# A chunked gated linear attention with an SSM projection: a reworked opening, and in the usual turns the third projection product moved ahead of the carried parts

## The chip, the cores and the metric

The kernel runs on one NeuronCore of a Trainium2 chip. It uses the five engines of that core: TensorE (PE, with its weight loads listed as PEld), VectorE (DVE), ScalarE (ACT), GpSimd (POOL) and SyncE (SP, which issues most transfers). The metric is the device time of one launch in microseconds (us); lower is better.

## What is computed

Two blocks in a row, all in float32. The first is a gated linear recurrence over 768 steps, for 4 batches and 8 heads of 48 numbers; the second projects its output to 2 × 512 columns, scans one half with a decay, gates it with the SiLU of the other half and projects back to 384 columns.

```python
for t in range(S):                                  # B, H, S, D = 4, 8, 768, 48
    state = alpha[:, :, t, :, None] * state + np.einsum('bhd,bhe->bhde', k[:, :, t], v[:, :, t])
    y[:, :, t] = np.einsum('bhd,bhde->bhe', q[:, :, t], state)
x = y.transpose(0, 2, 1, 3).reshape(B, S, H * D)    # (4, 768, 384)

proj = x @ w_in                                     # 384 x 1024
val, gate = proj[..., :512], proj[..., 512:]
a = np.exp(A_log)
for t in range(S):
    h = a[0, 0] * h + val[:, t, :]
    ys[:, t, :] = h
out = (gate * sigmoid(gate) * ys) @ w_out           # 512 x 384
```

The weights `w_in`, `A_log` and `w_out` come as numbers of 64 bits; the kernel turns their bits into float32 itself.

## The kernel before

The work is cut into 12 units of 256 steps (`GC`), three per batch. A unit `m` has an attention part and, one unit later, a projection part: turn `n` of the main loop does the attention of unit `m = n + 1` and the projection of unit `n`. The program's order is written out by hand (`manual_schedule`): each engine carries out its instructions in the order in which the code calls them, and semaphores make one engine wait for another.

**Attention of a unit.** alpha, k and q are loaded as `raw_a`, `raw_k`, `raw_q` (lines 410 and 421) and have to be turned, so that steps lie along the free axis. In the first units PE turns them by products with the identity (`turned`, line 694) or by transposes (lines 689 and 690) and ACT or DVE copy the result out of PSUM (`copy_turned`, lines 701 and 702); from unit 4 on DVE turns them by itself (`turn`, line 595). Two scans on DVE make the running products of alpha, forward (`scan_P`, L630) and backward (`scan_V`, L649); k and q are multiplied by them (`scaled_k` L614, `scaled_q` L605). Then PE does:

- `scores` (L744): k times q within each 64 steps, and k itself turned back; `masks` (L754 to L764) copies these out of PSUM, masked, by DVE, ACT and POOL;
- `values` (L778, for unit 0 `first_values`, L862): masked scores times v;
- `states` (L810): k times v, the step of the state for each 64 steps; `add_up` sums them on POOL (L828, L830), for the first units DVE does (L838, for unit 0 `first_states`, L879);
- `carried` (L791, for unit 0 `first_carried`, L870): q times the state at the start of each 64 steps, added to the values in the same PSUM banks (`y0`, `y1`);
- `join`: ACT copies the banks to `yst` (L904, L905), eight small transfers bring them into the layout `xT` (L907), ACT copies the rest straight (L909). For unit 0 `first_join` does this with four ACT copies.

**Projection of a unit.** `project(n, cc)` for `cc` from 0 to 3 makes 128 columns of values and 128 of gates on PE (L927, two PSUM banks), a scan with the decay on DVE (L932), a SiLU on ACT (L940) and their product on POOL (L942; DVE in the first turns). `output` is the last product (L956), its copy on ACT (L950) and two transfers.

**PSUM.** Four banks go round (`ps_mm`, tag `mm`), each given out again when its last reader is done: to the turned pieces, the second half of scores, each projection product (a pair), each output (a pair). Four more are named: `s0`, `s1`, `y0`, `y1`.

**Weights.** `load_w` brings the 64-bit numbers of `w_in` in three blocks (`units`: columns of product 0, of product 1, of products 2 and 3). `low(i)` (ACT, L544) takes the low word's bits, `convert(i)` the high word's on DVE (L553, L555) and adds the two on POOL (L557).

**The opening.** Before the loop unit 0 goes through alone: `keep_warm` (three products on zeros, L726), `alphas(0)` through the four named banks, q, k, `alphas(1)`, the scans, `turned(1, "k")`, scores, `turned(1, "q")`, masks, values, states, carried parts, join. Between them stand `low(0)`, `convert(0)`, `low(1)`, `convert(1)`. The loads on SP after the first ones are held back by a memset of one element on POOL (L1001) which stands behind the POOL add of `convert(0)`: `raw_a` of unit 2 must wait for it, and everything behind it on SP (the third weight block, k, q, alphas, v, the output weights) with it. `constants` (from L495) fills masks, paddings and the identity.

**A usual turn** (`n` from 2 on, the last `else` of the loop): scores and masks; product 0; values, states and three of the four sums (`second`); product 1; carried parts, values of the other half, join and the fourth sum (`third`), `load_v`; product 2; product 3; output of unit `n`. `go(count)` slips in steps of the DVE chain of unit `n + 2` (`products`).

Of the kernel before, what the change touches and what calls it, by code (L numbers as in the profile page):

```python
# [11 lines left out]
U32 = mybir.dt.uint32  # L12
# [334 lines left out]
def fast(  # L347
# [145 lines left out]
    def constants():  # L493
# [18 lines left out]
        for t in dS[0] + dS[1]:  # L512
            nc.vector.memset(t[:, :, :, D:64], 0.0)
        for t in sums:
            nc.vector.memset(t[:, :, D:64], 0.0)
        nc.vector.memset(K0[:, :, :, D:], 0.0)
# [21 lines left out]

    def low(i):
        bits, w = bits_of(i)  # L540
        r = p2.tile([C, UW], I32, tag="wr", name="wr")
        lows[i] = r.rearrange("p (a n) -> p a n", a=w.shape[1])
        halves = lows[i].bitcast(U16).rearrange("p a (n two) -> p a n two", two=2)
        nc.scalar.activation(halves[:, :, :, 0], bits[:, :, :, 0], AF.Copy, scale=2.0 ** -29)  # L544

    def convert(i):
        if i not in lows:
            low(i)
        bits, w = bits_of(i)
        r = lows.pop(i)  # L550
        halves = r.bitcast(U16).rearrange("p a (n two) -> p a n two", two=2)
        quarters = bits.rearrange("p a n two -> p a (n two)").bitcast(U16).rearrange("p a (n four) -> p a n four", four=4)
        nc.vector.tensor_scalar(out=w.bitcast(U32), in0=bits[:, :, :, 1], scalar1=3, scalar2=0x3FFFFFFF,  # L553
                                op0=ALU.logical_shift_left, op1=ALU.bitwise_and)
        nc.vector.tensor_scalar(out=halves[:, :, :, 1], in0=quarters[:, :, :, 3], scalar1=0xC000, scalar2=None,  # L555
                                op0=ALU.bitwise_and)
        nc.gpsimd.tensor_tensor(out=w.bitcast(I32), in0=w.bitcast(I32), in1=r, op=ALU.add)  # L557
# [125 lines left out]

    def turned(m, name, js, t):
        raw = steps_of(name, m)
        tp = t[:, 0:len(js) * C].rearrange("p (j x) -> p j x", j=len(js))
        if (m, name) in ((1, "k"), (1, "q"), (2, "a"), (3, "a")):
            for n, j in enumerate(js):
                nc.tensor.transpose(tp[:, n], raw[:, ds(ROW + j * D - 64, C)], ident)  # L689
                nc.tensor.transpose(tp[0:64, n], raw[:, ds(j * D, 64)], ident)  # L690
            return tp.rearrange("p j (c h) -> p h c j", h=4)
        for n, j in enumerate(js):
            for i in range(2):
                nc.tensor.matmul(tp[ds(64 * i, 64), n], raw[:, ds(i * ROW + j * D, 64)], ident,  # L694
                                 start=True, stop=True, skip_group_check=True)
        return tp.rearrange("p j (c h) -> p h c j", h=4)

    def copy_turned(to, js, tp, engine=None):
        place = by_runs(to)[:, :, :, js.start:js.stop]
        if engine:  # L700
            return engine.tensor_copy(out=place, in_=tp)
        return nc.scalar.activation(place, tp, AF.Copy)  # L702

    def turn_over(m, name, to, tags=(None, None)):
        size = NJ // len(tags)
        copies = []
        for n, tag in enumerate(tags):
            js = range(size * n, size * (n + 1))
            copy = copy_turned(to, js, turned(m, name, js, bank(tag)), nc.vector if n % 2 and tag else None)
            if tag:  # L710
                for other in copies[(n + 1) % 2::2]:
# [3 lines left out]
    def alphas(m, tags=(None, None)):  # L715
        turn_over(m, "a", by_place(als[m % 2])[:, :, 1:GP], tags)
# [31 lines left out]
    def masks(m):  # L748
        sc = [[t[:, 0:4 * (L + D)].rearrange("p (h x) -> p h x", h=4) for t in pair] for pair in scs.pop(m)]
        mb = mask[:, None, :]  # L750
        if m < NG:
            for c in range(G):
# [230 lines left out]
    alphas(0, ("s0", "s1", "y1", "y0"))  # L983
    tq = straighten(0, "q")
    tk = straighten(0, "k")
    alphas(1)
    P = scan_P(0)
    V = scan_V(0, P, False)
    halves = [range(0, NJ // 2), range(NJ // 2, NJ)]
    parts = [turned(1, "k", js, bank()) for js in halves]  # L990
# [22 lines left out]
    last = P[:, :, GC]  # L1013
    nc.scalar.activation(ratio[:, 0], last, AF.Copy, scale=1.0 / FIRST_PRODUCT)
    nc.scalar.activation(lower[:, :, 0], last, AF.Copy)
# [6 lines left out]
    first_carried((2, 3))  # L1022
    first_join()
    nc.scalar.activation(a_dec, a_log, AF.Exp)
# [26 lines left out]
    for n in range(N):  # L1051
# [70 lines left out]
        else:  # L1122
# [98 lines left out]
```

## Time and profile before

| | |
|---|---|
| median of 3 runs | 279.24 us (279.05 to 279.8) |
| profiled execution: its time | 279.67 us |
| its span, first to last instruction | 277.8 us |
| granted TensorE clock, mean | 1.000 |
| busy: PE, DVE, ACT, POOL | 271.7, 217.8, 110.3, 98.2 us |
| moved by DMA | 41.16 MB, 148 GB/s over the span |

The lines of the profile that follow are of three kinds. The chain of work that ended last has a start, a length and what ran. The timeline has a start, a length, engine, line of the code, operation, out<-in with shapes, a count, and in brackets the idle time before it with what ended it. A window over matmuls counts two rows for each product in float32. SPq is SyncE's queue of transfers; its length is that of the issue, and the landing is told apart.

### The profile page before, as it was taken

Reading aid. Unit: us, or ns where it says so; the run is one execution under the profiler, and the core shown is the slowest. Engines: PE = TensorE matmul, PEld = TensorE weight load, DVE = VectorE, ACT = ScalarE, POOL = GpSimd, SP = SyncE. Lnnn points to the kernel's source line nnn. Section 1 sums busy time; section 2 is a strip of 40 time slices with the busy share of each in tenths; the row PEclk is TensorE's granted clock in tenths of the full one; section 3 lists DMA queues with packets and bytes.
Section 4 is the critical chain, followed back from the end, with each engine's and each line's share of the span. In section 5 each row is a group of like instructions: output and inputs, shape, how many; then the busy total and the mean of one; then the engine's idle time right before and its main releaser. Section 6 shows DMA issues by size and latency. Waiting matters only on the chain.

```text
span 277.8 us, 9491 instructions
## 1 busy us (share of the span) xinstructions
PE 271.7 (98%) x4040; PEld 217.3 (78%) x4040; DVE 217.8 (78%) x281; ACT 110.3 (40%) x244; POOL 98.2 (35%) x105
## 2 busy tenths in 40 slices
PE   7999999999999999999999999999999999999995
PEld 5988987876688788788787787787787787787874
DVE  7889998898499599499499599499499598269640
ACT  2677763461325325325334334334343343341111
POOL 8131223230057155156156164164165163142000
PEclk9999999999999999999999999999999999999999
DMA  6949991935909739729659748829748711101101
GB/s 189 314 133 319 285 293 49 217 78 132 273 12 228 168 97 217 168 85 221 145 140 205 158 132 197 188 91 197 170 125 186 190 55 45 58 5 43 57 5 59
DMA packets 52462, 41.16 MB, mean 148 GB/s; under 512 B 27360, under 2 KB 50976, under 8 KB 52416
## 3 DMA queue, kind: packets, MB, share of 16 engines
q1 hardware_dynamic: 50768, 38.98, 55.3%
q10 hardware_dynamic: 1392, 0.99, 1.3%
q8 instruction: 32, 0.52, 0.8%
q0 software_dynamic: 256, 0.56, 0.7%
q14 instruction: 14, 0.11, 0.1%
HBM read 32.54 MB, written 4.72 MB: 134 GB/s over the span
## 4 chain that ended last, share of the span: by engine, by line
PE 94%; DVE 3%; DMA 1%; ACT 1%; issue 1%; SPq 0%; DVEq 0%; ACTq 0%
PE mm L927 47%; PE mm L956 20%; PE y L778 4%; PE y L791 4%; PE s L744 4%; PE mm L744 3%; PE s L810 3%; PE mm L1182 2%; DMA raw_a<-in_alpha_dram 1%; PE mm L694 1%; PE mm L689 1%; PE mm L690 1%; DVE V L649 1%; DVE P L630 1%; PE y L862 1%; PE s L694 1%
## 5 line engine op out<-in xcount | busy, mean ns | idle before, releaser
L927 PE MATMUL mm<-xT,w_in 128*128 128x256 f32 x576 | 133.4, 385 | 0.6 <-ACT xT L884 0.6
L927 PEld LDWEIGHTS mm<-xT,w_in 128*128 128x128 f32 x576 | 106.7, 190 | 17.1 <-issue 0.8
L956 PE MATMUL mm<-w_out,f_last 128*128 128x384 f32 x160 | 53.2, 486 | 0.0
L940 ACT ACTIVATE sg<-mm 128x256 f32<-128x256 f32 x48 | 18.4, 384 | 72.4 <-PE mm L927 71.9
L956 PEld LDWEIGHTS mm<-w_out,f_last 128*128 128x128 f32 x160 | 30.4, 190 | 19.1
L942 POOL TENSOR_TENSOR f_last<-sg,hh 128x256 f32<-128x256 f32 x36 | 34.3, 954 | 24.7 <-ACT sg L940 21.2
L830 POOL TENSOR_TENSOR sum<-sum,dS 128x192 f32<-128x192 f32 x30 | 31.2, 1039 | 18.2 <-ACT dS L818 16.8
L762 POOL TENSOR_TENSOR AK<-AK,mask 128x512 f32<-128x512 f32 x9 | 11.5, 1281 | 67.4 <-ACT AK L760 67.4
L649 DVE TENSOR_TENSOR_SCAN V<-al,ends 128x1028 f32<-128x1028 f32 x12 | 30.1, 2512 | 0.4
L932 DVE TENSOR_TENSOR_SCAN hh<-a_dec,hh,mm 128x256 f32<-128x256 f32 x32 | 23.1, 722 | 8.3 <-PE mm L927 8.1
L950 ACT ACTIVATE o_sb<-mm 128x384 f32<-128x384 f32 x22 | 10.8, 491 | 46.4 <-PE mm L956 46.4
L630 DVE TENSOR_TENSOR_SCAN P<-al,lower 128x1028 f32<-128x1028 f32 x12 | 27.5, 2292 | 0.4
L759 DVE TENSOR_TENSOR A<-s,mask 128x256 f32<-128x256 f32 x9 | 3.8, 425 | 29.5 <-PE s L744 29.5
L595 DVE STREAM_TRANSPOSE k<-raw_k 128x1024 f32<-128x1024 f32 x9 | 18.3, 2033 | 0.0
L595 DVE STREAM_TRANSPOSE q<-raw_q 128x1024 f32<-128x1024 f32 x9 | 18.1, 2016 | 0.0
L557 POOL TENSOR_TENSOR w_in<-w_in,wr 128x768 int32<-128x768 int32 x4 | 7.3, 1832 | 26.4 <-ACT al L702 9.5
L595 DVE STREAM_TRANSPOSE al<-raw_a 128x1024 f32<-128x1024 f32 x8 | 16.4, 2048 | 0.1
L605 DVE TENSOR_TENSOR Zq<-q,P 128x1024 f32<-128x1024 f32 (+1 forms) x14 | 15.0, 1070 | 0.3
L778 PEld LDWEIGHTS y<-AK,v 64*64 64x64 f32 x352 | 12.1, 134 | 3.6 <-issue 3.6
L614 DVE TENSOR_TENSOR Zk<-k,V 128x1024 f32<-128x1024 f32 (+1 forms) x14 | 14.7, 1050 | 0.1
L778 PE MATMUL y<-AK,v 64*64 64x64 f32 x352 | 14.5, 221 | 0.0
L778 PE MATMUL y<-A,v 64*64 64x64 f32 x352 | 14.5, 221 | 0.0
(158 smaller groups left out, 375.1 us busy)
## 6 DMA issues: line engine op xcount, KB each, us to landing
v<-in_v_dram SPq DMA_DIRECT2D x22, 192.0 KB, 4.0
out_dram<-o_sb SPq DMA_DIRECT2D x22, 192.0 KB, 4.2
raw_k<-in_k_dram SPq DMA_DIRECT2D x18, 184.0 KB, 3.6
raw_q<-in_q_dram SPq DMA_DIRECT2D x18, 184.0 KB, 4.2
raw_k<-in_k_dram SPq DMA_DIRECT2D x18, 176.0 KB, 4.1
raw_q<-in_q_dram SPq DMA_DIRECT2D x18, 176.0 KB, 4.3
raw_a<-in_alpha_dram SPq DMA_DIRECT2D x16, 184.0 KB, 5.2
raw_a<-in_alpha_dram SPq DMA_DIRECT2D x16, 176.0 KB, 5.1
```

The lines of the kernel that those rows point to most:

```text
L595: nc.vector.transpose(out=by_runs(to).rearrange("p h c j -> p h j c"), in_=raws[name][:, 0:4 * ROW].rearrange("p (h j d) -> p h j d", h=4, ...
L605: nc.vector.tensor_mul(Zqs[m % 2][:, ds(u0, n), :, D:].rearrange("p u h t -> p h u t"), t[:, :, at].rearrange("p h (u t) -> p h u t", t=L) ...
L630: nc.vector.tensor_tensor_scan(out=P, data0=al[:, 0:4 * GP], data1=lower.rearrange("p h t -> p (h t)"), initial=0.0, op0=ALU.mult, op1=ALU ...
L649: nc.vector.tensor_tensor_scan(out=V[:, ::-1], data0=al[:, 1:4 * GP + 1][:, ::-1], data1=ends.rearrange("p h t -> p (h t)")[:, ::-1], init ...
L744: nc.tensor.matmul(scs[m][c][i][ds(L * h, L), ds(p * (L + D), L + D)], Zk[rows, c, p, ds(h * L, L)], Zq[rows, u, p], start=True, stop=True ...
L778: nc.tensor.matmul(ys[m][i][ds(64 * s, 64), e, ds(c * C + h * L, L)], v_sb[rows, c, 4 * i + p, :], As[i][rows, c, p, :], start=across and ...
L830: nc.gpsimd.tensor_add(Ss[j][:, :, 0:D], Ss[j - 1][:, :, 0:D], part)
L927: nc.tensor.matmul((pv, pg)[vg], w_ins[cc][:, kk, vg, :], xT[:, kk, :], start=(kk == 0), stop=(kk == NK - 1))
L932: nc.vector.tensor_tensor_scan(out=hh, data0=a_dec[:, cc:cc + 1].to_broadcast([C, GC]), data1=pv, initial=prev_h[cc][:, GC - 1:GC] if n % ...
L940: nc.scalar.activation(sg, pg, AF.Silu)
L942: f = lambda: engine.tensor_mul(fs[n][cc], sg, hh)
L956: nc.tensor.matmul(os[c], fs[n][cc][:, ds(c * C, C)], w_outs[cc // 2][:, cc % 2, :], start=(cc == 0), stop=(cc == NI - 1))
```

## The change

Two parts. In the opening:

- `constants` leaves out the memsets of the paddings of `dS`, `sums` and `K0`; those of `sums` come back on POOL, later.
- `first_alphas` turns the alphas of unit 0 by 32 products of 64 × 64 (each with a quarter of the identity) in place of 16 of 128 × 64; four copies out as before, on ACT and DVE.
- `first_q` turns q of unit 0 with the order of the products changed: first all eight of the half that ACT's queue loads, then all eight of the other half.
- k of unit 0 and the alphas of unit 1 are turned by transposes (`turned_by_transpose`) in place of products.
- `turned(1, "k")` is split: one half before the scores, one after them. `turned(1, "q")` is split: one half after the states, one after the last carried parts.
- `masks` for unit 0 comes before all conversion of weights; `convert` is split into `high` (DVE), `low` (ACT) and `add_low` (POOL), and `low(0)` stands behind the copies of the scores, `high(1)` is done in two halves.
- The copies of P's last column (`ratio`, `lower`) on ACT come right after `scan_P(0)`.

In the usual turns `third(m)` and `load_v(m + 2)` come after `project(n, 2)` and its gating product; they came before.

```diff
@@ constants @@
-        for t in dS[0] + dS[1]:
-            nc.vector.memset(t[:, :, :, D:64], 0.0)
-        for t in sums:
-            nc.vector.memset(t[:, :, D:64], 0.0)
-        nc.vector.memset(K0[:, :, :, D:], 0.0)
@@ low, convert @@
+    def high(i, part=slice(None)):
         bits, w = bits_of(i)
+        halves = room(i)[1][:, part]
...
+        nc.vector.tensor_scalar(out=w.bitcast(U32)[:, part], in0=bits[:, part, :, 1], scalar1=3, scalar2=0x3FFFFFFF,
+                                op0=ALU.logical_shift_left, op1=ALU.bitwise_and)
+        nc.vector.tensor_scalar(out=halves[:, :, :, 1], in0=quarters[:, part, :, 3], scalar1=0xC000, scalar2=None,
+                                op0=ALU.bitwise_and)
+
+    def add_low(i):
+        w = bits_of(i)[1]
+        nc.gpsimd.tensor_tensor(out=w.bitcast(I32), in0=w.bitcast(I32), in1=lows.pop(i), op=ALU.add)
@@ turned @@
+    turned_by_transpose = ((0, "k"), (1, "a"), (1, "k"), (1, "q"), (2, "a"), (3, "a"))
...
-        if (m, name) in ((1, "k"), (1, "q"), (2, "a"), (3, "a")):
+        if (m, name) in turned_by_transpose:
@@ new @@
+    def first_alphas():
+        raw, to = steps_of("a", 0), by_runs(by_place(als[0])[:, :, 1:GP])
+        tps = [[bank(tag)[:, 0:NJ // 2 * 64].rearrange("p (j x) -> p j x", x=64) for tag in tags]
+               for tags in (("s0", "s1"), ("y1", "y0"))]
+
+        def turn_quarter(j, i, r):
+            rows = ds(64 * r, 64)
+            nc.tensor.matmul(tps[j // 4][r][ds(64 * i, 64), j % 4], raw[rows, ds(i * ROW + j * D, 64)],
+                             ident[rows, rows], start=True, stop=True, skip_group_check=True)
+
+        for j in range(2):
+            for r in range(2):
+                turn_quarter(j, 1, r)
+        for j in range(NJ):
+            for r in range(2):
+                turn_quarter(j, 0, r)
+                if j + 2 < NJ:
+                    turn_quarter(j + 2, 1, 1 - r)
...
+    def first_q():
+        raw, to = steps_of("q", 0), plain("q")
+        tps = [bank().rearrange("p (j x) -> p j x", x=C) for _ in range(2)]
+        for i in (1, 0):
+            for j in range(NJ):
+                nc.tensor.matmul(tps[j // 4][ds(64 * i, 64), j % 4], raw[:, ds(i * ROW + j * D, 64)], ident,
+                                 start=True, stop=True, skip_group_check=True)
...
@@ the opening @@
-    alphas(0, ("s0", "s1", "y1", "y0"))
-    tq = straighten(0, "q")
+    first_alphas()
+    tq = first_q()
     tk = straighten(0, "k")
     alphas(1)
     P = scan_P(0)
+    last = P[:, :, GC]
+    nc.scalar.activation(ratio[:, 0], last, AF.Copy, scale=1.0 / FIRST_PRODUCT)
+    nc.scalar.activation(lower[:, :, 0], last, AF.Copy)
     V = scan_V(0, P, False)
-    parts = [turned(1, "k", js, bank()) for js in halves]
+    part = turned(1, "k", halves[0], bank())
     for c in range(G):
         scaled_k(0, tk, V, c)
         scaled_q(0, tq, P, c)
-    scores(0)
     tk = plain("k")
-    for js, part in zip(halves, parts):
-        copy_turned(tk, js, part)
+    copy_turned(tk, halves[0], part)
+    for c in range(G):
+        scores(0, (c,))
+    part = turned(1, "k", halves[1], bank())
+    for c in range(G):
+        masks(0, (c,))
+    copy_turned(tk, halves[1], part)
+    high(0)
+    high(1, slice(0, None, 2))
     low(0)
-    parts = [turned(1, "q", js, bank()) for js in halves]
-    convert(0)
+    add_low(0)
     nc.gpsimd.memset(raws["a"][0:1, 0:1], 0.0)
     load_steps("a", 2, [nc.sync])
     load_w(units[2], nc.sync)
-    masks(0)
-    low(1)
     first_values(True)
     st = states(0)
-    convert(1)
+    tq = plain("q")
+    part = turned(1, "q", halves[0], bank())
     first_states(st)
-    tq = plain("q")
-    for js, part in zip(halves, parts):
-        copy_turned(tq, js, part)
...
+    low(1)
+    copy_turned(tq, halves[0], part)
+    high(1, slice(1, None, 2))
+    add_low(1)
+    for t in sums:
+        nc.gpsimd.memset(t[:, :, D:64], 0.0)
...
     first_carried((2, 3))
+    part = turned(1, "q", halves[1], bank())
     first_join()
+    copy_turned(tq, halves[1], part)
@@ the usual turn @@
-            third(m)
-            load_v(m + 2, nc.sync)
             go(1)
             f2 = project(n, 2)
             f2()
+            third(m)
+            load_v(m + 2, nc.sync)
```

More of the change, by code (lines that the diff above doesn't have):

```diff
@@ L548, in convert @@
             low(i)
[L549 to L557, printed above, removed]
+        high(i)
+        add_low(i)
     def check_w(i):
@@ L696, in turned @@
         return tp.rearrange("p j (c h) -> p h c j", h=4)
[L698 to L705, printed above, removed]
-        copies = []
[L707 to L711, printed above, removed]
+    halves = [range(0, NJ // 2), range(NJ // 2, NJ)]
@@ L718, in straighten, with turn_over, alphas @@
+    def turn_over(m, name, to):
+        for js in halves:
+            copy_turned(to, js, turned(m, name, js, bank()))
+    def alphas(m):
+        turn_over(m, "a", by_place(als[m % 2])[:, :, 1:GP])
     def straighten(m, name):
```

35 lines of the change are left out of this document (22 added, 13 removed).

## The prediction

> **What bounds the kernel now.** I read the page first (parts 1 and 4), then the chain of work, then the timelines by engine.
>
> ```profile
> PE 271.7 (98%) x4040; PEld 217.3 (78%) x4040; DVE 217.8 (78%) x281; ACT 110.3 (40%) x244; POOL 98.2 (35%) x105
> ...
> PE 94%; DVE 3%; DMA 1%; ACT 1%; issue 1%; SPq 0%; DVEq 0%; ACTq 0%
> ```
>
> TensorE (PE) is busy 98% of the span and carries 94% of the chain that ended last. A time can therefore only come out of work that PE does, or out of the few microseconds in which PE stands still. The chain over one usual turn (n = 8):
>
> ```profile
> 202.97 2.79 PE mm L927 x12
> 205.76 0.39 PE y L791 x16
> ...
> 207.08 5.38 PE mm L927 x24
> 212.46 5.16 PE mm L956 x16
> 217.62 0.93 PE s L744 x32
> ...
> 259.02 7.77 PE mm L927 x36
> ```
>
> Second projection product, carried parts (three pieces, 205.76 to 207.08), third and fourth product together, output, next scores: each piece begins where the last one ends. No usual turn has an idle PE. The idle time is in the opening.
>
> **The usual turns: third product ahead of the carried parts.** PE's instructions stay the same and change places: two products in one run (5.38) now stand before the carried parts, one (2.79) behind them. 2.79 + 5.38 is the sum on both sides, so PE's work is unchanged: 0. What could break this is a wait. The other engines in the same turn, by the timeline:
>
> ```profile
> 201.11 0.69 DVE L932 TENSOR_TENSOR_SCAN hh<-a_dec,hh,mm 128x256 f32<-128x256 f32 x1
> 201.72 0.38 ACT L940 ACTIVATE sg<-mm 128x256 f32<-128x256 f32 x1 [1.80 <-PE mm L927]
> 207.27 2.60 POOL L830 TENSOR_TENSOR sum<-sum,dS 128x192 f32<-128x192 f32 x1
> 207.63 0.59 ACT L905 ACTIVATE yst<-y 128x512 f32<-128x512 f32 x1
> 210.69 1.56 POOL L942 TENSOR_TENSOR f_last<-sg,hh 128x256 f32<-128x256 f32 x1 [0.82 <-DVE hh L932]
> 210.75 5.34 SPq L907 DMA_DIRECT2D xT<-yst  x8
> ...
> 249.16 4.95 SPq L907 DMA_DIRECT2D xT<-yst  x8
> ```
>
> and, of the tile xT in the stretch from 197 to 220:
>
> ```profile
> DMA to landing us min/median/max: 1.9/3.1/4.9
> ```
>
> - The third product takes over the PSUM pair of the first. Its two readers (scan, Silu) end at 202.1; the product now wants the pair at 205.76. Covered by 3.6 us.
> - The fourth sum moves behind the third gating product on POOL: that one ends at 212.25, the sum at worst takes its 2.60 again (214.85), and the fourth gating product then ends about 1.6 later, 216.4. The output needs it after 6 of 8 products, 212.46 + 6 × 0.645 = 216.3. So the cover holds even nearly at the worst; with the sum out of the way of the scan it is likelier to be about 1 us long. 0.
> - The join (copies to yst, eight transfers) starts 2.6 to 2.8 later. But SP reached it only at 210.75, because eight loads of k and alpha stand ahead; the second yst copy ended at 208.22 and now ends near 211.0. So SP's transfers move by some 0.3 to 0.5, not by 2.7. The last of the eight issues (5.34 in all) goes out at about 215.5 and lands 1.9 later, 217.4; the next turn's first product starts after two halves of scores, 217.62 + 0.93 and about 0.8, 219.3. Some 1.4 of cover is left. load_v and the raw_q load behind it on SP move by as little and are wanted a turn later. Where no raw loads stand ahead (n = 9 and 10) the join moves the whole 2.7: in n = 10 from 249.16 to 251.9, its last issue to about 256.3, its landing to 258.2; the next product starts at 259.02.
>
> So this half of the change is worth 0, from −0.2 to +1 over the nine turns.
>
> **The opening, on PE.** Idle memsets leave DVE, the alphas of unit 0 are turned in quarters, q in a new order, k and the alphas of unit 1 by transposes, and halves of k(1) and q(1) stand later.
>
> ```profile
> 4.72 1.80 PE L694 MATMUL s<-ident,raw_a 128*64 128x128 f32 x16 [0.36 <-DMA raw_a<-in_alpha_dram]
> 6.34 1.05 PE L694 MATMUL y<-ident,raw_a 128*64 128x128 f32 x16
> 7.21 1.93 PE L694 MATMUL mm<-ident,raw_q 128*64 128x128 f32 x32
> 8.96 1.93 PE L694 MATMUL mm<-ident,raw_k 128*64 128x128 f32 x32
> ...
> 12.56 0.33 PE L689 MATMUL mm<-ident,raw_k 128*128 128x128 f32 x1
> ...
> 14.46 1.00 PE L744 MATMUL s<-Zq,Zk 48*64 48x112 f32 x32
> 15.64 1.00 PE L744 MATMUL mm<-Zq,Zk 48*64 48x112 f32 x32 [0.18 <-ACT k L702]
> 16.57 0.33 PE L689 MATMUL mm<-ident,raw_q 128*128 128x128 f32 x1
> ...
> 18.80 0.22 PE L862 MATMUL y<-AK,wide 64*64 64x64 f32 x1
> 18.81 0.22 PE L862 MATMUL y<-A,wide 64*64 64x64 f32 x1
> 18.86 0.22 PE L862 MATMUL y<-AK,wide 64*64 64x64 f32 x1
> ...
> 23.49 5.42 PE L927 MATMUL mm<-xT,w_in 128*128 128x256 f32 x24 [0.56 <-ACT xT L884]
> ```
>
> (Each f32 product shows as two rows.)
>
> *Alphas in quarters.* Before, PE is free of keep_warm at 4.36 (4.72 less its wait of 0.36) and q starts at 7.21. The first 16 rows step by 0.10 (PE still slow: the next 16 step by 0.054), so the speed doubles near 6.3. Quarters have half the rows and half the columns, four side by side. Eight rows of one half can start as keep_warm ends, 4.4; the rest, 48 rows four at a time at 0.107 and 8 at two, end near 6.45. −0.76.
>
> *q in the order "all of half 1, then all of half 0".* In the old order halves alternate, and 32 rows take 8.96 − 7.21 = 1.75, 0.055 a row. A 256-column row of L927 takes 0.216, so 128 columns alone take 0.108: the 0.055 is two column halves side by side. The rows at 18.80 and 18.86 show what the same tile does with itself: the next one starts 0.055 later, just the length of 64 columns; nothing overlaps. In the new order eight products in a row go to the same half, so 32 rows take 0.108 each, 3.5. +1.75. (Bounds: 0 if they overlapped after all, +1.75.)
>
> *k(0) and alphas(1) by transposes.* 16 transposes of L689/L690 took from 12.56 to about 14.4, 1.8, against 1.75. 0, at most +0.1.
>
> *Halves of k(1), q(1).* PE's work is the same, but each return to transposes costs a start: after 16.57 the second one begins 0.16 later and the following ones every 0.11. Two halves instead of one piece make about three such starts more, +0.45.
>
> The Trainium skill (TensorEngine Tiling (Array Packing), Key Properties) says that a change of tiling mode drains TensorE. By it alone the extra changes of mode (quarters to halves, four in and out of the transposes) would each cost something; the 0.16 above agrees, and the sum stands on that row.
>
> *Idle time that goes.* 0.18 ahead of the second scores, about 0.2 ahead of the carried parts, 0.56 ahead of the first projection (now half of q(1) is turned there): −0.94.
>
> Sum at the first projection product: −0.76 + 1.75 + 0.45 − 0.94 = +0.5, i.e. 24.0 instead of 23.49. PE has no slack left to hide more.
>
> **The opening, on the others.**
>
> ```profile
> 8.04 2.30 DVE L630 TENSOR_TENSOR_SCAN P<-al,lower 128x1028 f32<-128x1028 f32 x1
> 14.81 0.69 DVE L605 TENSOR_TENSOR Zq<-q,P 128x512 f32<-128x512 f32 x1
> 15.96 1.08 ACT L544 ACTIVATE wr<-wbits 128x768 uint16<-128x768 uint32 x1
> 17.18 1.83 POOL L557 TENSOR_TENSOR w_in<-w_in,wr 128x768 int32<-128x768 int32 x1 [9.06 <-DVE AK L754]
> 17.82 0.33 ACT L756 ACTIVATE dS<-mm 128x192 f32<-128x192 f32 x1
> 19.06 1.19 SPq L421 DMA_DIRECT2D raw_a<-in_alpha_dram  x2
> 28.66 1.09 ACT L544 ACTIVATE wr<-wbits 128x768 uint16<-128x768 uint32 x1 [1.23 <-DMA wbits<-in_moe_w_in_dram]
> 29.61 0.35 ACT L940 ACTIVATE sg<-mm 128x256 f32<-128x256 f32 x1
> 29.88 0.67 ACT L702 ACTIVATE al<-mm 128x512 f32<-128x512 f32 x1
> 31.40 0.95 PE L744 MATMUL mm<-Zq,Zk 48*64 48x112 f32 x32
> 34.08 1.92 PE L694 MATMUL mm<-ident,raw_q 128*64 128x128 f32 x32
> ```
>
> DVE: the scan P starts near 7.3, not 8.04, because the alphas are done 0.76 sooner, and V, as long, ends near 12.15; but k is only turned at 11.9 and copied (0.67, as the copy at 29.88) at 12.6 because q took longer on PE, so Zk and Zq move by only −0.3 and are no longer what the scores wait for. The eleven memsets that go had kept DVE from the copies by little, and six come back on POOL, idle there; the copies of P's last column on ACT come into a wait of ACT; the second half of the second block's conversion on DVE comes after the state sums, over 4 us before its product: 0 together, ±0.1.
>
> Weights: low(0) on ACT moves from 15.96 to behind the four copies after the scores and the second k(1) copy. Scores end near 16.45 (16.57 before), masks 17.3, last copy (0.33) 17.7, k copy (0.6) 18.25, low(0) 19.3, the POOL add (1.83) 21.1. The memset of one element that gates SP's next loads stands behind that add: raw_a(2) starts at about 21.2 instead of 19.06, +2.1, and with it the third weight block behind it on SP. ACT waited for that block until 28.66; now until about 30.7 (bounds: +1.2, if the block, started later, finds emptier queues, to +2.1). Queued behind that wait on ACT are the Silu of the second product, the copies of alphas(2), low(3) and the copies after scores(1).
>
> Who waits for them: the second half of scores(1) needs the PSUM bank that this Silu frees. 30.7 + 1.09 + 0.35 = 32.15 at the earliest, against 31.40 before and 31.9 by PE's own +0.5. Behind it two alpha copies (0.6 each), low(3) (1.0) and three copies (0.3 each) end at about 35.0, and the turning of q(2) takes over one of those banks: 35.0 instead of 34.08. So PE is late by 0.8 to 1.0 after this point, of which 0.5 was lost already. From there every stretch is PE's work, and the lateness stays to the end.
>
> **Sum.** 0 (usual turns) + 0.5 + 0.35 = +0.85 on the profiled execution's 279.67 (span 277.8, 1.87 around it): 280.5. That execution lies 0.43 above the median of the runs, 279.24, so against the median: 280.1. Own range of this case +0.4 to +1.2: 279.6 to 280.5.
>
> **Rivals.**
> 1. *The late block is hidden* (not slower). If the block lands only 1.2 later (29.8), Silu ends at 31.2, before PE asks, and the copies end at 34.1. Then only PE's +0.5 counts, less whatever the 0.45 for starts was sized too high: 279.3 to 279.7. For it: the block's issues would meet no earlier load in the queue. Against: the same loads follow it at the same pace, and the block needed 8 us from issue to landing. It decides when the gate moves by less than 1.5. Chance 0.24.
> 2. *q's halves overlap* (faster). Then PE is ready for the scores at 12.8 and the scores wait for Zq at 13.65; PE's work up to the projection shrinks by 1.75 and the gate moves by only 1.5. At the best, with no new idle time, the projection starts at 22.3: 278.1; with the idle time ahead of the scores it starts at 23.3 and the time is 279.0. Against: the rows at 18.80 to 18.86. Chance 0.12.
> 3. *The clock falls while PE transposes.* After the change k(0), alphas(1) and half of k(1) are 4.4 us of transposes without a product in between; the longest such stretch before was 1.8. If PE went back to the half speed that it had until 6.3, about 4.5 us would run at half speed, some 2.2 lost: 282.3. The transposes before kept 0.11 each to the end of their stretch, so nothing here speaks for it but the length. The Trainium skill (TensorE: Matmul & The Clock Gate, Part 4) says that transposes do not count as busy for the clock gate; no row here shows a stretch long enough to test it. Chance 0.07.
> 4. *The join is late in the usual turns.* If SP's eight transfers moved the whole 2.7, the last would land at 220.1, 0.9 after the product wants it, in up to seven turns: 285. Against: SP gets there at 210.75 either way. Chance 0.03.
>
> **Chances.** Forecast 0.54, rivals 0.24, 0.12, 0.07, 0.03. A measurement of this kernel can tell about 0.3% (0.84; its three runs span 0.75) from no change, so the bounds are 278.4 and 280.1, and the forecast lies on the upper one. Of the forecast's 0.54 I put 0.35 above it and 0.19 within; rival 1 within (0.20) or just above (0.04); rival 2 splits 0.08 faster, 0.04 within; rivals 3 and 4 are slower. Slower 0.49, same 0.43, faster 0.08. For 8 in 10: 278.9 to 281.1.
>
> **What would show each step.** q's 32 rows take 3.5 (else 1.75); the first projection starts at 24.0; SP's raw_a(2) issue stands at 21.2; ACT's third low waits until 30.7; a PE wait appears ahead of scores(1)'s second half or of q(2), and none appears in the usual turns, whose length stays 20.5. The prediction fails if q overlaps, if the block lands before 30, or if a usual turn grows.

## The result, and the profile after

The changed kernel takes 281.24 us (median of 22 runs, 279.17 to 282.44) where the kernel before takes 279.56 beside it (22 runs, 278.76 to 280.88). The ratio is 1.0046, with a 95% interval of 1.0029 to 1.0063: slower by 1.3 us (0.8 to 1.8). Ratios and intervals, here and below, are worked out from the single runs without the one slow execution among them (285.88 us, of the last kernel but one in the table below), and not from the medians, which here lie 1.68 apart. On the 279.24 of the forecast that is 280.5; the forecast was 280.1, from 278.9 to 281.1. The direction and the size were right. The place was only half right, and that the sum came so close is luck, as the section on the prediction shows.

The page of the changed kernel, its busy times and the shares of the chain that ended last:

```profile
PE 272.9 (98%) x4040; PEld 217.7 (78%) x4040; DVE 217.8 (78%) x272; ACT 109.5 (39%) x244; POOL 91.1 (33%) x111
...
PE 82%; DVE 8%; DMA 5%; issue 2%; SPq 1%; ACTq 0%; ACT 0%; DVEq 0%
```

The shares say where to look. PE's part of the chain fell from 94% to 82%, and what took its place is DVE with 8% and DMA with 5%. The chain of work of the changed kernel shows that PE comes into it only at 45.34, and that from there on a usual turn is as it was:

```profile
9.86 9.02 DMA wbits<-in_moe_w_in_dram
...
45.34 0.41 PE s L781 x4
...
74.94 0.93 PE s L781 x32
...
80.77 5.38 PE mm L964 x24
86.14 0.39 PE y L828 x16
...
87.47 2.79 PE mm L964 x12
90.26 5.16 PE mm L993 x16
95.42 0.93 PE s L781 x32
```

A turn takes 95.42 − 74.94 = 20.48 us, as forecast: the 5.38 of two products stands ahead of the carried parts, the 2.79 behind them, nothing waits. All of the loss is in the opening. The chain there goes through the landing of the second weight block (`wbits`, from 9.86 to 18.88) and from then on through VectorE, not through PE.

The timeline of the kernel before, around the same place (VectorE, GpSimd's addition to block 1, and PE's first product of unit 1):

```profile
18.19 1.26 DVE L553 TENSOR_SCALAR w_in<-wbits 128x768 uint32<-128x768 uint32 x1 [0.40 <-DMA wbits<-in_moe_w_in_dram]
...
20.11 1.83 POOL L557 TENSOR_TENSOR w_in<-w_in,wr 128x768 int32<-128x768 int32 x1 [1.08 <-DVE wr L555]
...
20.82 0.36 DVE L879 TENSOR_TENSOR wide_S<-mm,wide_S 128x192 f32<-128x192 f32 x1
...
21.75 2.35 DVE L630 TENSOR_TENSOR_SCAN P<-al,lower 128x1028 f32<-128x1028 f32 x1
24.14 0.17 DVE L646 TENSOR_TENSOR ratio<-P,ends 128x4 f32<-128x4 f32 x1
...
24.55 2.30 DVE L649 TENSOR_TENSOR_SCAN V<-al,ends 128x1028 f32<-128x1028 f32 x1
...
43.68 0.68 DVE L605 TENSOR_TENSOR Zq<-q,P 128x512 f32<-128x512 f32 x1
...
45.98 2.86 PE L927 MATMUL mm<-xT,w_in 128*128 128x256 f32 x12
```

and the timeline of the changed kernel, all engines, in order of time:

```profile
5.93 3.33 PE L742 MATMUL mm<-ident,raw_q 128*64 128x128 f32 x32
...
18.25 1.83 POOL L554 TENSOR_TENSOR w_in<-w_in,wr 128x768 int32<-128x768 int32 x1 [10.14 <-ACT wr L541]
...
18.90 1.46 DVE L547 TENSOR_SCALAR w_in<-wbits 128x384 uint32<-128x384 uint32 x1 [1.62 <-DMA wbits<-in_moe_w_in_dram]
...
20.29 1.19 SPq L421 DMA_DIRECT2D raw_a<-in_alpha_dram  x2
...
21.79 0.42 DVE L547 TENSOR_SCALAR w_in<-wbits 128x384 uint32<-128x384 uint32 x1
...
22.45 2.29 DVE L633 TENSOR_TENSOR_SCAN P<-al,lower 128x1028 f32<-128x1028 f32 x1
22.71 3.63 POOL L554 TENSOR_TENSOR w_in<-w_in,wr 128x768 int32<-128x768 int32 x1 [2.45 <-DVE wr L549]
23.01 2.75 PE L964 MATMUL mm<-xT,w_in 128*128 128x256 f32 x12
...
24.77 1.59 DVE L649 TENSOR_TENSOR ratio<-P,ends 128x4 f32<-128x4 f32 x1
...
26.39 2.86 PE L964 MATMUL mm<-xT,w_in 128*128 128x256 f32 x12 [0.63 <-POOL w_in L554]
26.61 2.30 DVE L652 TENSOR_TENSOR_SCAN V<-al,ends 128x1028 f32<-128x1028 f32 x1
...
29.61 0.33 PE L694 MATMUL mm<-ident,raw_a 128*128 128x128 f32 x1 [0.36 <-DVE hh L969]
29.89 1.10 ACT L541 ACTIVATE wr<-wbits 128x768 uint16<-128x768 uint32 x1 [2.75 <-DMA wbits<-in_moe_w_in_dram]
30.84 0.36 ACT L977 ACTIVATE sg<-mm 128x256 f32<-128x256 f32 x1
...
31.86 1.00 PE L781 MATMUL s<-Zq,Zk 48*64 48x112 f32 x32 [0.28 <-DVE Zq L608]
32.68 0.95 PE L781 MATMUL mm<-Zq,Zk 48*64 48x112 f32 x32
...
45.71 0.69 DVE L608 TENSOR_TENSOR Zq<-q,P 128x512 f32<-128x512 f32 x1
...
47.53 2.86 PE L964 MATMUL mm<-xT,w_in 128*128 128x256 f32 x12
```

What the reader is to see:

- At the first projection product PE is at 23.01, half a microsecond ahead of before (23.49). What is lost is lost behind it, most of it in three waits of PE: for GpSimd's addition to block 1 (0.63), for the scan `hh` (0.36), for `Zq` (0.28). Another follows at 45.34.
- VectorE stands idle for 1.62 at 18.90 until block 1 has landed; in the kernel before it waited 0.40 for the same block. There the whole conversion stood ahead of the state sums and of the scan P(1). Now one half stands ahead of the sums, the other between the sums and P(1) (21.79), and P(1) starts 0.70 late. The first half takes 1.46 where the second takes 0.42: it ends 0.28 after GpSimd's addition for block 0 (18.25 + 1.83 = 20.08).
- GpSimd's addition for block 1 waits for the second half of the conversion and so starts at 22.71 instead of 20.11, beside P(1) instead of ahead of it, and needs 3.63 instead of 1.83. `ratio`, a product of 128 × 4 numbers, takes 1.59 where it took 0.17. It ends at 26.36, the addition at 26.34.
- So V(1) starts at 26.61 instead of 24.55, 2.06 late, and as VectorE has no gap up to Zq(2), that one starts 2.03 late (45.71 against 43.68). Of the 2.06, 0.70 is the later start of P(1) and 1.42 is `ratio` (P(1) itself was 0.06 shorter).
- The first projection product of unit 1 is 1.55 late (47.53 against 45.98). From there to the end every kernel profiled here takes 231.8 to 231.9 us, so the whole difference arises ahead of that product.

### The profile page after: what moved, and what is told of

Same layout as the page of the kernel before. It is cut to its first block, busy times and chain, and to the rows that moved or that the text cites. A ratio compares the mean times of both kernels' runs of the same rounds, so it can differ in the third digit from the quotient of the medians.

```text
span 279.4 us, 9488 instructions
## 1 busy us (share of the span) xinstructions
PE 272.9 (98%) x4040; PEld 217.7 (78%) x4040; DVE 217.8 (78%) x272; ACT 109.5 (39%) x244; POOL 91.1 (33%) x111
## 4 chain that ended last, share of the span: by engine, by line
PE 82%; DVE 8%; DMA 5%; issue 2%; SPq 1%; ACTq 0%; ACT 0%; DVEq 0%
PE mm L964 44%; PE mm L993 20%; PE y L815 4%; PE y L828 4%; PE s L781 3%; DMA wbits<-in_moe_w_in_dram 3%; PE mm L781 3%; PE s L847 3%; PE mm L1227 2%; DMA raw_k<-in_k_dram 2%; DVE P L633 2%; DVE V L652 1%; DVE hh L969 1%; DVE Zq L608 1%; DVE ratio L649 1%
## 5 line engine op out<-in xcount | busy, mean ns | idle before, releaser
L979 POOL TENSOR_TENSOR f_last<-sg,hh 128x256 f32<-128x256 f32 x36 | 37.0, 1028 | 34.2 <-DVE hh L969 15.9
L867 POOL TENSOR_TENSOR sum<-sum,dS 128x192 f32<-128x192 f32 x30 | 18.9, 629 | 18.2 <-ACT dS L855 16.8
L554 POOL TENSOR_TENSOR w_in<-w_in,wr 128x768 int32<-128x768 int32 x4 | 9.1, 2279 | 26.0 <-ACT wr L541 16.8
L781 PEld LDWEIGHTS s<-Zq,Zk 48*64 48x64 f32 x384 | 9.6, 132 | 6.6 <-PE mm L993 4.9
```

What stands on the lines that cost most here:

```text
L781: nc.tensor.matmul(scs[m][c][i][ds(L * h, L), ds(p * (L + D), L + D)], Zk[rows, c, p, ds(h * L, L)], Zq[rows, u, p], start=True, stop=True ...
L867: nc.gpsimd.tensor_add(Ss[j][:, :, 0:D], Ss[j - 1][:, :, 0:D], part)
L979: f = lambda: engine.tensor_mul(fs[n][cc], sg, hh)
```

## Experiments

Three theories. **VectorE theory:** the chain on VectorE from P(1) to Zq(2) is what PE waits for. **Block theory** (the forecast's): q in the serial order and the late third weight block, by way of ACT's Silu. **Turn theory:** the usual turns. One measure is used beside the times: the stretch on PE from the start of the first scores to the start of the third projection product of unit 0. It leaves out what happens before the scores, which varies from run to run (last section). But it ends ahead of the wait at 45.34, so the last column gives the stretch up to the first projection product of unit 1 as well. The medians in the table come from 10 to 12 runs of each kernel (22 of the changed one), the ratios are against the kernel before, the starts are from one profile each.

| kernel | median us | ratio (95% interval) | scores start | third product | stretch | to unit 1 |
|---|---|---|---|---|---|---|
| before | 279.6 | 1 | 14.46 | 35.92 | 21.46 | 31.52 |
| changed | 281.24 | 1.0046 (1.0029 to 1.0063) | 13.71 | 37.20 | 23.49 | 33.82 |
| third product moved alone | 279.42 | 0.9988 (0.9973 to 1.0004) | 14.12 | 36.06 | 21.94 | 31.53 |
| opening alone | 280.58 | 1.0030 (1.0009 to 1.0050) | 14.06 | 37.31 | 23.25 | 33.42 |
| no addition to block 1 | 280.52 | 1.0035 (1.0022 to 1.0047) | 13.84 | 36.82 | 22.98 | 32.76 |
| P(1) early | 280.71 | 1.0040 (1.0023 to 1.0057) | 13.47 | 36.92 | 23.45 | 32.89 |
| q alternating | 280.99 | 1.0024 (1.0002 to 1.0045) | 13.51 | 37.11 | 23.60 | 33.78 |
| early release | 280.83 | 1.0046 (1.0025 to 1.0068) | 13.84 | 37.04 | 23.20 | 33.37 |
| P(1) early, early release | 280.49 | 1.0019 (1.0004 to 1.0033) | 14.76 | 37.40 | 22.64 | 32.43 |
| the same, block 1 behind the sums | 279.09 | 0.9984 (0.9967 to 1.0001) | 14.60 | 35.91 | 21.31 | 30.91 |
| the same, q alternating | 278.93 | 0.9969 (0.9946 to 0.9992) | 13.04 | 34.74 | 21.70 | 31.96 |
| block 1 behind the sums, P(1) early, old release | 281.47 | 1.0078 (1.0044 to 1.0112) | 13.42 | 37.58 | 24.16 | 33.77 |
| before, P(1) early | 280.05 | 1.0001 (0.9975 to 1.0027) | 14.19 | 35.74 | 21.55 | 31.73 |

### The two halves of the change

```diff
 # e1, on the kernel before                      # e2, on the changed kernel: the reverse
-            third(m)
-            load_v(m + 2, nc.sync)
             go(1)
             f2 = project(n, 2)
             f2()
+            third(m)
+            load_v(m + 2, nc.sync)
```

> The opening of before with only the third product moved ahead of the carried parts in the usual turns. Three theories of the +1.3 us. VectorE theory: the loss comes from VectorE's chain in the opening, so this kernel gives before's time, 0.0 +- 0.3 us, with a turn of 20.5. Block theory (the forecast's: q serial on PE and the late third weight block, both in the opening): the same 0.0. Turn theory: the loss, or a part of it, comes from the usual turns; then +0.5 to +1.3 here, and in the profile a wait of PE in the turns. GpSimd's state sums should fall from a mean near 1.04 us to about 0.63 under every theory.

> The new opening, with the usual turns as they were before. VectorE theory and block theory: the whole loss is here, +1.3 us against before (+0.8 to +1.8). Turn theory: +0.0 to +0.8.

The third product moved alone gives 0.9988, no loss. The opening alone gives 1.0030, and its stretch is nearly that of the changed kernel (23.25 against 23.49). Turn theory falls. GpSimd's groups in the kernel with the third product moved:

```profile
L830 POOL TENSOR_TENSOR sum<-sum,dS 128x192 f32<-128x192 f32 x30 | 19.1, 638 | 18.3 <-ACT dS L818 16.8
```

and in the kernel with the opening alone:

```profile
L867 POOL TENSOR_TENSOR sum<-sum,dS 128x192 f32<-128x192 f32 x30 | 30.9, 1029 | 18.3 <-ACT dS L855 16.8
```

The state sums fall from 1.03 to 0.64 us each when the third product is moved ahead of them, 12 us of GpSimd's time in all. That is worth nothing measurable, since GpSimd is not what anyone waits for there.

### Without GpSimd's addition to block 1

This kernel leaves out the low bits of 256 of the columns of `w_in`.

```diff
-    add_low(1)
+    lows.pop(1)
```

> The changed kernel without GpSimd's addition of the low bits of weight block 1, so those 256 columns of w_in keep their high words alone: that part of the computation is left out. VectorE theory: the small product for ratio, which took 1.59 us because it could not end before that addition did, takes about 0.17 again; VectorE's chain up to Zq(2) is 1.4 us earlier, and PE's wait of 0.6 for the addition goes too: about 1.0 to 1.4 us faster than the changed kernel, so +0.0 to +0.3 against before. Block theory: the third weight block lands as late as in the changed kernel (29.9), so nothing moves: +1.3.

The timeline of this kernel:

```profile
25.21 0.17 DVE L649 TENSOR_TENSOR ratio<-P,ends 128x4 f32<-128x4 f32 x1
...
30.70 1.09 ACT L541 ACTIVATE wr<-wbits 128x768 uint16<-128x768 uint32 x1 [3.13 <-DMA wbits<-in_moe_w_in_dram]
...
31.70 1.36 PE L781 MATMUL mm<-Zq,Zk 48*64 48x112 f32 x32
```

`ratio` takes 0.17 again, so the addition was what held it. But of the 1.0 to 1.4 us expected, only 0.3 arrives (1.0035 against 1.0046, the intervals overlap), and the stretch shortens by 0.5. In the trace the rest arrives later: up to unit 1 it is 1.06 (32.76 against 33.82). The last two rows show a second limit: ACT waits for the third block until 30.70 and the second half of the scores takes 1.36 instead of 0.95, held up in the middle. Close behind the limit of the VectorE theory stands the limit of the block theory.

### P(1) early

```diff
     high(0)
+    P = scan_P(1)
     high(1, slice(0, None, 2))
...
-    P = scan_P(1)
     first_carried((1,))
```

> The changed kernel with scan_P(1) right behind high(0) on VectorE, ahead of the wait for weight block 1 and of the state sums. The scan then starts near 17.3 instead of 22.45 and V(1) near 22.3 instead of 26.6. VectorE theory: Zq(2) comes 2 us or more earlier, the PE waits for VectorE at scores(1) and scores(2) go, and the lateness goes with them until something else binds: at the least back to before's time (0.0), at best -1.0; the state sums move by +1 us at most. Block theory: the third block still lands at 29.9 and holds ACT, so the +1.3 stays or falls by no more than 0.4. If both hold, the block is what binds next: PE's wait then shows ahead of scores(1)'s second half or q(2), at -0.2 to +0.3.

Timeline of this kernel:

```profile
18.04 2.79 POOL L554 TENSOR_TENSOR w_in<-w_in,wr 128x768 int32<-128x768 int32 x1 [9.92 <-ACT wr L541]
...
21.03 1.19 SPq L421 DMA_DIRECT2D raw_a<-in_alpha_dram  x2
...
21.74 1.15 PE L907 MATMUL y<-Zq,wide_S 48*64 48x64 f32 x48 [1.12 <-DVE wide_S L916]
...
30.79 1.10 ACT L541 ACTIVATE wr<-wbits 128x768 uint16<-128x768 uint32 x1 [2.91 <-DMA wbits<-in_moe_w_in_dram]
...
32.16 0.99 PE L781 MATMUL mm<-Zq,Zk 48*64 48x112 f32 x30 [0.22 <-ACT sg L977]
```

No clear gain (1.0040); the number is the block theory's, for other reasons than in the changed kernel. VectorE's waits at the scores are gone. In their place: the scan holds up GpSimd's addition for block 0 (2.79 instead of 1.83), so SyncE's loads are released at 21.03 instead of 20.29 and the third block comes at 30.79 instead of 29.89; the Silu behind it holds PE at 32.16; and the state sums, still behind block 1's conversion, hold PE for 1.12 at 21.74.

### q alternating

```diff
-        for i in (1, 0):
-            for j in range(NJ):
+        for j in range(NJ):
+            for i in (1, 0):
```

> The changed kernel with the 32 rows of q(0) alternating between the two column halves again. The forecast's step (PE has no slack in the opening): q takes 1.75 again instead of 3.33, and the time falls by 1.3 to 1.75 against the changed kernel, so to between -0.3 and 0.0 against before. VectorE theory: PE turns q in 1.75 all right and the scores come some 0.5 to 1 us sooner (Zk and Zq then set their start), but VectorE still waits for weight block 1 until 18.9 and its chain from P(1) on starts where it did; PE only waits longer ahead of the projection and of scores(1): less than 0.4 faster than the changed kernel, +0.8 to +1.5 against before.

The waits of PE in this kernel:

```profile
PE s L781 <- DVE Zq L608: 1.0, 3, 0.5
PE mm L964 <- POOL w_in L554: 0.6, 1, 0.6
PE mm L694 <- DVE hh L969: 0.4, 1, 0.4
```

These waits are those of the changed kernel, with one more for Zq ahead of the first scores; the third product starts at 37.11 against 37.20, the first of unit 1 at 47.29 against 47.53. In the trace the order of q is worth little here: what PE wins it waits. (q itself started 0.54 later in this execution, at 6.47, so the trace may hide a part.) The ratio is 0.6 us lower (1.0024 against 1.0046), just below what the VectorE theory expected and above the forecast's range; the intervals overlap, and the times alone don't decide.

### Releasing SyncE's loads early

```diff
+    nc.gpsimd.tensor_copy(out=raws["a"][0:1, 0:1], in_=w_ins[0][0:1, 0, 0, 0:1])
     add_low(0)
-    nc.gpsimd.memset(raws["a"][0:1, 0:1], 0.0)
```

> The changed kernel with the one-element write that holds back SyncE's loads moved ahead of GpSimd's addition for block 0; it copies one element of high(0)'s result, so it goes out near 17.2 instead of 20.1, and the third weight block lands about 2 to 2.8 us sooner than 29.9. VectorE theory: VectorE's chain binds, not the block, so the time stays within 0.3 of the changed kernel's: +0.9 to +1.5 against before. Block theory: ACT is free earlier and the lateness at scores(1) and q(2) goes: +0.3 to +0.6 against before.

Timeline of this kernel:

```profile
27.39 1.08 ACT L541 ACTIVATE wr<-wbits 128x768 uint16<-128x768 uint32 x1 [0.42 <-DMA wbits<-in_moe_w_in_dram]
...
31.70 1.00 PE L781 MATMUL s<-Zq,Zk 48*64 48x112 f32 x32 [0.29 <-DVE Zq L608]
```

The third block lands 2.5 us sooner (27.39 against 29.89) and the time is the same, 1.0046 (the two intervals together leave about 0.8 us either way; the stretch to unit 1 is 0.45 shorter). In the changed kernel as it is, the third block is not what binds first. The block theory falls as the main cause of this loss, though not as a limit, as the next runs show.

### Both, and the wait for block 1 taken away

```diff
 # e12: P(1) early and the early release. e13: besides, block 1 in one piece behind the sums
     high(0)
-    high(1, slice(0, None, 2))
+    P = scan_P(1)
...
     first_states(st)
...
-    high(1, slice(1, None, 2))
+    high(1)
```

> Both edits together: scan_P(1) right behind high(0), and the one-element write ahead of the addition for block 0. Alone the early scan left scores(2) at 44.39 (45.34 in the changed kernel, 43.40 in before), with PE waiting 0.22 for the Silu behind the third block. If there are two limits, VectorE's chain and the third block, each hiding the other, this kernel loses both: scores(2) near 43.4 or sooner, time -0.3 to +0.3 against before. If the block is no limit (VectorE theory alone), it stays where the early scan alone was, +0.4 to +1.1.

> As the kernel with both edits, and in addition weight block 1's conversion on VectorE in one piece behind the state sums. The sums then need not wait for the block's landing (18.9) and its conversion: PE's wait of 1.1 ahead of the last carried parts goes, the first projection product starts near 23.0 instead of 23.75. Two limits theory: 0.5 to 0.8 faster than the kernel with both edits, -1.0 to -0.3 against before. If something on PE itself binds (q in the serial order, the starts of the transposes), it stays at about the time of the kernel with both edits.

> The kernel with the early scan and block 1's conversion behind the sums, but with the one-element write back behind GpSimd's addition for block 0, as in the changed kernel. Two limits theory: the third block lands near 30 again and ACT's Silu behind it holds up scores(1)'s second half and q(2) by 0.5 to 1: +0.2 to +0.7 against before, where the same kernel with the early write gave -0.5. If only VectorE's chain mattered: the same as with the early write, -0.5.

With both edits the ratio falls to 1.0019 and the stretch to 22.64; either edit alone had left it at 1.0040 and 1.0046. What is left in its profile, apart from the wait before the first instruction, is 1.12 for the state sums. With block 1's conversion behind the sums that goes too: 0.9984, stretch 21.31. The waits of PE in that kernel, complete:

```profile
PE y L763 <- DVE raw_q L498: 1.4, 1, 1.4
```

Only the wait before the first instruction is left, which every kernel here has. The numbers that two limits led one to expect of the two kernels (−0.3 to +0.3, then −1.0 to −0.3) were met by the second (−0.45) and missed by the first, which came out at +0.5, in the range of the VectorE theory alone; its expectation overlooked the sums, which the kernel with P(1) early had shown. The step between them, 1.0, is more than the 0.5 to 0.8 expected.

The last run of the three is the counter-test. It is the same kernel with the old release. Timeline:

```profile
31.46 1.08 ACT L541 ACTIVATE wr<-wbits 128x768 uint16<-128x768 uint32 x1 [4.97 <-DMA wbits<-in_moe_w_in_dram]
...
32.82 0.99 PE L781 MATMUL mm<-Zq,Zk 48*64 48x112 f32 x30 [2.27 <-ACT sg L977]
```

ACT waits 4.97 for the third block, and PE 2.27 for the Silu behind it. The time is 1.0078 (1.0044 to 1.0112), 2.6 us above the same kernel with the early release and more than the +0.2 to +0.7 expected. This is the forecast's mechanism, laid bare. It is larger here than in the changed kernel, since the early scan also holds up GpSimd's addition for block 0 and the block lands at 31.46 instead of 29.89.

Four kernels show that there are two limits, VectorE's chain and the third block: the changed one (1.0046), with the early release alone (1.0046), with VectorE's chain shortened alone (1.0078), and with both (0.9984). Either edit alone gains nothing in the time; both together gain 0.62%. Two things stay open. No kernel has block 1 behind the sums without the early scan, so how much each of these two does was not separated. And in the traces the single edits are not without effect: up to unit 1 the early scan is worth 0.93, the early release 0.45, and the two together 1.39, about their sum. The times can't tell such gains from none.

### q alternating where PE has no waits, and P(1) early in the kernel before

> The kernel with the early scan, the early release of SyncE's loads and block 1's conversion behind the sums (0.9984 of before), and in addition q(0)'s rows alternating between the column halves. In that kernel's profile PE waits for nobody from the first scores on, so now PE's own work should count. Forecast's step (the serial order costs PE time): q takes about 1.75 instead of 3.3, k is turned and copied sooner, Zk starts 0.3 to 0.8 sooner and with it everything behind it: 0.3 to 0.9 us faster than without, so -1.4 to -0.8 against before. If VectorE's scans P and V set the start of the scores anyway: no gain, -0.5 against before.

Timeline:

```profile
6.63 1.96 PE L742 MATMUL mm<-ident,raw_q 128*64 128x128 f32 x30 [0.37 <-DMA raw_q<-in_q_dram]
...
13.04 1.00 PE L781 MATMUL s<-Zq,Zk 48*64 48x112 f32 x32
```

30 rows of q take 1.96, against 3.33 for 32 in the serial order, and the scores start at 13.04. The row also shows what the serial order bought: the half of q that lands last is wanted 0.37 before it is there. The median is 278.93 and the ratio 0.9969 (0.9946 to 0.9992): faster than the kernel before by 0.9 us, and the fastest of the kernels tried. That is within the expected −1.4 to −0.8. But against the same kernel with serial q (0.9984) the gain is 0.4 and the intervals overlap, so it is not shown; and the stretch to unit 1 is longer (31.96 against 30.91), so a part of the earlier start is lost again.

```diff
 # e9, on the kernel before
     P = scan_P(0)
+    last = P[:, :, GC]
+    nc.scalar.activation(ratio[:, 0], last, AF.Copy, scale=1.0 / FIRST_PRODUCT)
+    nc.scalar.activation(lower[:, :, 0], last, AF.Copy)
...
-    convert(1)
+    P = scan_P(1)
     first_states(st)
+    convert(1)
...
-    P = scan_P(1)
```

> The kernel before with scan_P(1) ahead of the state sums and of block 1's conversion, and the two small copies that it needs on ACT right behind scan_P(0); nothing else. In before VectorE's chain from P(1) (21.75) to Zq(2) has no gap, and scores(2) starts as the last pieces of Zq(2) come out. If VectorE's chain bound before too, this is 0.3 to 0.7 faster than before. If the third block (Silu behind its landing at 28.66) and PE's own work bind it, the same within 0.2; if the scan ahead of the sums holds up the carried parts, +0.3 to +1.

1.0001: nothing. Its V(1) shows why:

```profile
23.63 3.83 DVE L649 TENSOR_TENSOR_SCAN V<-al,ends 128x1028 f32<-128x1028 f32 x1
```

V(1) starts 0.92 sooner than before (24.55), but now beside GpSimd's addition, and takes 3.83 instead of 2.30. It ends 0.6 later. There was hardly an idle moment on VectorE to win in the kernel before; only the order changed. Whether VectorE's chain bound there too, this run doesn't settle, since its V(1) became later.

## Why the prediction was right, and where it was not

- **Usual turns, 0: right.** 20.48 a turn, no wait of PE, and the half alone measures 0.9988.
- **q in the serial order, +1.75: the size right, the effect not.** 32 rows take 3.33 (3.5 forecast), against 2.30, and 1.96 for 30 rows, in the alternating order at the same place. But "PE has no slack left to hide more" was wrong: from the first projection product on PE waits four times, 0.28 to 0.63 each, for VectorE and GpSimd, and undoing the order alone moves the third product by 0.09 in the trace.
- **Opening on PE, +0.5 at the first projection product: wrong by 1.0.** It started at 23.01, not 24.0. Half of that is PE's speed at the start: q started at 5.93 instead of the 6.45 forecast, since PE reached full speed sooner in this execution (the alphas' rows take 0.22 from 5.18 on) than in the one read for the forecast, where the rows' step halved near 6.3. Of the rest, 0.24 is q (3.26 to the next row, not 3.5). The split of k(1) and q(1) was sized rightly but counted too often: a half takes 1.02 (15.40 to 16.42) where eight steps of 0.11 are 0.88, so 0.14 for each of two more pieces, not three. The row that the forecast read, 0.16 against 0.11, shows only 0.05 of it.
- **Late third weight block, +0.35: the mechanism right, not the binding one.** By the prediction's own sign ("if the block lands before 30") this step failed. The release moved by 1.23 (20.29), not 2.1, since the first scores and the copies behind them came about a microsecond sooner than the forecast had them; the block landed at 29.89, not 30.7. As a limit it exists: in the two kernels with the early scan and the old release PE waits 0.22 and 2.27 for the Silu, though in them the block lands later still (30.79 and 31.46). In the changed kernel PE asks for that bank only after Zq, later than the Silu ends (31.2 against 32.68).
- **The others, "0 together, ±0.1": this step failed.** It asked when the second half of block 1's conversion is wanted by its own product, and not what stands behind it on VectorE: that is P(1), 0.70 late. And GpSimd's addition, which waits for this half, moves from 20.11 to 22.71, beside P(1), and `ratio` then costs 1.42 more; without the addition it takes 0.17 and the stretch to unit 1 is 1.06 shorter. Together V(1) is 2.06 late, which arrives as +1.55 at the first projection product of unit 1 and stays to the end.
- **Rival 1** (the block hidden, not slower) had its condition met (the release moved by less than 1.5) and still gave the wrong time, since the chain on VectorE was in no rival. **Rival 2** fell: q's rows of the same half don't overlap. **Rival 3** fell: 40 transposes in a row (9.19 to 13.71) kept their 0.11. **Rival 4** fell: a turn stayed at 20.48.

The sum of +0.85 came close to +1.3 by luck. Its larger term, +0.5 on PE, measured −0.48; its other term, +0.35, didn't bind; the loss came from the term put at 0.

## What to carry to other kernels

When two engines both run late by about the same, undoing either may show nothing in the time; test the pair, and test each with the other taken away. Before a move is priced at nothing, look along the queue of the engine that it is moved on for what stands behind it, and at what waits for it elsewhere: here half a conversion was put right ahead of a scan, and the addition on GpSimd that waits for this half came to lie beside that scan. An addition on GpSimd is not always free for VectorE; place it beside work of PE and ACT, not beside VectorE's chain.

## What the hardware showed that was not expected

**GpSimd and VectorE can exclude each other.** In the changed kernel P(1) started first and kept its 2.29, GpSimd's addition took 3.63 (1.83 alone), and `ratio` then took 1.59 and ended with it. Where the addition started first, the scan V took 3.83 instead of 2.30, 1.53 more. The Trainium skill (SBUF — State Buffer, "SBUF: two separate sides") says that the port pair which the two share is an exclusive lock, between a GpSimd instruction that reads SBUF and a VectorE one that has two inputs in SBUF or runs in one of its two-port modes: whoever starts first has it for the whole instruction, and the other blocks. These rows agree, down to an operation of four columns. So do the state sums, which read one input from PSUM: in the kernel before the sum at 20.82 took 0.36 in the middle of GpSimd's addition (20.11 to 21.94), and in the changed kernel, with no addition running, the same sum takes 0.36 too (21.05).

**PE's half speed at the start ends at another time in each run.** The timeline of the kernel with both edits and block 1 behind the sums, whose program is the changed kernel's up to the first scores:

```profile
6.46 3.69 PE L742 MATMUL mm<-ident,raw_q 128*64 128x128 f32 x32
...
14.60 1.00 PE L781 MATMUL s<-Zq,Zk 48*64 48x112 f32 x32
```

In the changed kernel q starts at 5.93, takes 3.33, and the scores start at 13.71. In the kernel before, the first 16 rows of the alphas take 1.80; in the kernel with the third product moved alone, whose opening is the same, 1.09. Over the eight kernels with these same instructions the first scores start between 13.42 and 14.76. The granted clock in the profile's windows is 1.00 throughout, so it is the rows' own step that shows it. The Trainium skill (TensorE: Matmul & The Clock Gate, Part 1) says that the window by which the speed is raised runs freely and isn't tied to the kernel's start, that the point where the speed rises varies by ±500 ns, and that the number of slow products varies from run to run. The scores' spread of 1.3 us agrees in kind and is somewhat wider; that all of it comes from there was not shown. It means that one profile's start says little; a stretch between two events behind it says more. Whether it is also why the changed kernel's times spread further (3.3 us against 2.1) was not tested.
